# Whole-tile output stores, and v loads issued from ScalarE's queue, in a fused linear-attention and FFN kernel

## The chip, the cores and the metric

The kernel runs on one core of a Trainium2 chip. The metric is device time in microseconds, as the median of several runs. Below, "the profile" is one traced run of a kernel; its span is some 2 us shorter than the time of the same run, because the time includes the start and end of the launch. TensorE is PE, VectorE DVE, ScalarE ACT, GpSimd POOL, SyncE SP; a "q" after the name is the engine's sequencer.

## The reference

```python
# q, k, v: (4, 8, 768, 64) float32; lam: (8,)
for b in range(12):                       # blocks of 64 tokens
    intra = (qb @ kb.T * Dmask) @ vb      # decayed causal attention inside the block
    inter = (qb * lam_pow) @ kv_state     # what earlier blocks left
    out[:, :, sl] = intra + inter
    kv_state = lam_block * kv_state + (kb * rev_pow).T @ vb
x = out.transpose(0, 2, 1, 3).reshape(3072, 512)
h = x @ w_in                              # 512 -> 2048
g = h + sin(alpha * h) ** 2 / (alpha + 1e-9)
return g @ w_out                          # (3072, 512) float32
```

## The kernel before

The attention is cut into 24 units u (a batch row, four heads, 256 tokens); four units make a group g of 512 tokens for the FFN, and a group gives four output tiles (g, m) of 128 rows by 512 columns. The order of all work is fixed by a long list of items such as `ld.12.2:S` (the v load of unit 12 on SyncE) or `st.3.1.0:S` (the store of half 0 of tile 3.1). Each engine takes its own items strictly in order.

The parts that matter here:

```python
stagep = ...tile_pool(name="stage", bufs=8)     # q, k, v as loaded
outp   = ...tile_pool(name="outp", bufs=4)      # output tiles "ob"

def load(u, j, **_):
    ...
    loads[u, j] = nc.sync.dma_start(out=tl[:]..., in_=src[b, ...]...)

def outev(u, c, eng, **_):                      # attention output -> xt, tokens as (two, i)
    copy(eng, xt[g][:, 2 * hh:2 * hh + 2, bb, c, :],
         okv[u][c][:, 0:2 * P].rearrange("p (hp i) -> p hp i", hp=2))

def out_rows(g, m):
    ...
    return out[r0:r0 + C].rearrange("(p two) d -> two p d", two=2)   # (2, 64, 512)

def store(g, m, par, **_):                      # twice per tile
    nc.sync.dma_start(out=out_rows(g, m)[par],
                      in_=obs[g, m][par * D:(par + 1) * D, :])
```

Partitions 0 to 63 of an output tile hold the even rows, 64 to 127 the odd ones. Therefore a tile goes out in two stores, each to every second row.

## Time and profile before

| | before |
|---|---|
| median time | 215.98 us (216.06 with the run added beside the change) |
| span of the profile | 213.8 us |
| TensorE busy | 204.0 us, 95% |
| DMA issues from SyncE for output | 46 of 128 KB, and the last tile's pieces |
| first tile of group 4 copied at | 184.4 us; from there to the end 29.4 us |

The busy share says how full an engine is over the whole span; the chain says what the end depended on. Here TensorE is full, so a change elsewhere can help little. For the comparison I divide the span at the start of the copy of output tile 4.0 (read from VectorE's timeline): what lies ahead of it is called the middle, what follows it the tail.

### The profile page before, as it was taken

The numbers are of one execution on the slowest core, as the hardware profiler recorded it, in microseconds if no ns is written. First come the engines' busy times: TensorE is split into PE (matmuls) and PEld (weight loads), VectorE is DVE, ScalarE is ACT, GpSimd is POOL, SyncE is SP. The second block draws the span as 40 slices with busy tenths as digits, with TensorE's granted clock in tenths as the row PEclk, the third lists the DMA queues.
The fourth block names the chain that finished last, engine by engine and source line by source line (L and its number), as shares of the span: only waits on it lengthen the run. The fifth ranks groups of instructions, "written<-read, shape, count | busy, mean of one in ns | idle before, by whom it ended". The sixth has DMA issues, their size and how long they took to land.

```text
span 213.8 us, 5465 instructions
## 1 busy us (share of the span) xinstructions
PE 204.0 (95%) x2104; PEld 110.1 (51%) x2132; DVE 129.8 (61%) x235; ACT 123.5 (58%) x244; POOL 141.4 (66%) x208
## 2 busy tenths in 40 slices
PE   7989999999999999999799999999999999999993
PEld 5767544457744554455444554454454444444463
DVE  3885798159599845778667785626884626441120
ACT  3563984077899839986394496936635659131001
POOL 5488389689797999999898996709841728030000
PEclk9999999999999999999999999999999999999999
DMA  5999999999999999989899997520610000171624
GB/s 144 293 235 196 187 204 271 282 291 289 200 205 202 248 213 289 208 103 199 218 268 133 223 179 198 92 49 0 132 44 3 0 0 0 35 179 35 147 51 98
DMA packets 64009, 33.92 MB, mean 159 GB/s; under 512 B 19680, under 2 KB 61040, under 8 KB 63984
## 3 DMA queue, kind: packets, MB, share of 16 engines
q1 hardware_dynamic: 59568, 29.31, 62.5%
q0 software_dynamic: 4224, 4.19, 12.4%
q8 instruction: 16, 0.26, 0.5%
q10 hardware_dynamic: 192, 0.07, 0.2%
q14 instruction: 9, 0.07, 0.1%
HBM read 27.28 MB, written 6.29 MB: 157 GB/s over the span
## 4 chain that ended last, share of the span: by engine, by line
PE 67%; POOL 12%; DMA 10%; issue 3%; ACT 2%; SPq 2%; DVE 2%; POOLq 0%; ACTq 0%
PE ops L525 27%; PE hps L482 24%; DMA w_out_sb<-in_moe_w_out_dram 4%; PE bz L564 3%; DMA QT<-KD 2%; PE okv L460 2%; POOL KD L300 2%; POOL kvbd L425 2%; PE sp L368 2%; PE bz L588 2%; DMA st_v<-in_v_dram 2%; POOL QL L300 2%; POOL kvx L421 2%; PE pt L327 2%; SPq L259 2%
## 5 line engine op out<-in xcount | busy, mean ns | idle before, releaser
L482 PE MATMUL hps<-xt,w_in_sb 128*128 128x512 bf16 (+1 forms) x404 | 86.4, 362 | 0.6 <-issue 0.2
L525 PE MATMUL ops<-w_out_sb,gall 128*128 128x512 bf16 x352 | 83.2, 379 | 2.1 <-issue 1.3
L516 DVE SCALAR_TENSOR_TENSOR gall<-s,r_sb,hps 128x512 bf16<-128x512 bf16 x96 | 68.3, 744 | 23.3 <-POOL s L511 11.7
L502 ACT ACTIVATE s<-hps,alpha_sb 128x512 bf16<-128x512 f32 x96 | 63.2, 688 | 25.7 <-PE hps L482 25.1
L482 PEld LDWEIGHTS <-w_in_sb 128*128 128x128 bf16 x416 | 39.8, 98 | 40.6
L511 POOL TENSOR_TENSOR s<-s 128x512 bf16<-128x512 bf16 x35 | 36.3, 1045 | 36.3 <-ACT s L502 35.6
L525 PEld LDWEIGHTS <-gall 128*128 128x128 bf16 x368 | 34.6, 98 | 39.9 <-issue 0.6
L378 DVE TENSOR_TENSOR ST<-sp,mask 128x512 bf16<-128x512 f32 x48 | 31.9, 684 | 4.4 <-PE sp L368 4.2
L509 ACT ACTIVATE s<-s 128x512 bf16<-128x512 bf16 x51 | 31.6, 634 | 1.0 <-DVE gall L516 0.4
L284 DVE COPY ob<-ops 128x512 f32<-128x512 f32 (+1 forms) x13 | 8.6, 659 | 29.2 <-PE ops L525 23.6
L300 POOL TENSOR_TENSOR QL<-st_q,E 128x512 bf16<-128x512 f32 x23 | 23.9, 1042 | 3.6 <-DVE alpha_sb L574 2.2
L300 POOL TENSOR_TENSOR KD<-st_k,R 128x512 bf16<-128x512 f32 x22 | 22.9, 1042 | 3.5 <-DMA st_k<-in_k_dram 1.8
L425 POOL TENSOR_TENSOR kvbd<-kvx,LBD 128x256 bf16<-128x256 f32 x32 | 19.6, 612 | 2.5
L282 ACT COPY ob<-ops 128x512 f32<-128x512 f32 (+2 forms) x13 | 7.1, 547 | 22.4 <-PE ops L550 12.0
L282 ACT CAST xt<-okv 128x256 bf16<-128x256 f32 x29 | 9.8, 374 | 11.8 <-PE okv L460 11.8
L421 POOL TENSOR_TENSOR kvx<-kva,kvs 128x128 f32<-128x128 f32 x32 | 14.7, 460 | 1.2 <-ACT kva L282 1.0
L284 DVE CAST xt<-okv 128x256 bf16<-128x256 f32 x19 | 7.7, 420 | 11.5 <-PE okv L460 11.5
L282 ACT COPY kva<-kvp 128x128 f32<-128x128 f32 x26 | 6.4, 273 | 9.9 <-PE kvp L400 8.9
L368 PE MATMUL sp<-QT 64*64 64x128 bf16 x384 | 9.9, 219 | 1.3 <-DMA QT<-KD 1.3
L282 ACT COPY QT<-pt 128x512 bf16<-128x512 bf16 x9 | 5.2, 591 | 9.8 <-PE pt L327 9.7
L460 PE MATMUL okv<-ST,VB 64*64 64x128 bf16 x384 | 9.9, 220 | 0.0
L282 ACT CAST VB<-st_v 128x512 bf16<-128x512 f32 x14 | 8.6, 625 | 1.9 <-DMA st_v<-in_v_dram 1.8
(57 smaller groups left out, 127.1 us busy)
## 6 DMA issues: line engine op xcount, KB each, us to landing
st_q<-in_q_dram SPq DMA_DIRECT2D x24, 256.0 KB, 4.8
st_k<-in_k_dram SPq DMA_DIRECT2D x24, 256.0 KB, 5.0
st_v<-in_v_dram SPq DMA_DIRECT2D x24, 256.0 KB, 4.6
out_dram<-ob SPq DMA_DIRECT2D x46, 128.0 KB, 2.8
w_in_sb<-in_moe_w_in_dram POOLq DMA_DIRECT2D x4, 512.0 KB, 7.7
w_out_sb<-in_moe_w_out_dram POOLq DMA_DIRECT2D x4, 512.0 KB, 11.9
QT<-QL SPq DMA_TRANSPOSE x16, 4.1
QT<-KD SPq DMA_TRANSPOSE x16, 3.4
```

Source lines behind the costliest of these rows:

```text
L282: nc.scalar.copy(out=out, in_=in_)
L284: eng.tensor_copy(out=out, in_=in_)
L300: eng.tensor_tensor(out=t[:], in0=stage[u, j][:].rearrange("p h two e -> p two h e"), in1=tab[:, :, hh * HH:(hh + 1) * HH].unsqueeze(3).to ...
L378: nc.vector.tensor_tensor(out=stm[u][:, hd], in0=sps[u][hd][:], in1=mask[:].unsqueeze(2).to_broadcast([P, 2, 2, P]), op=ALU.mult)
L421: eng.tensor_tensor(out=t[:], in0=x, in1=prev[:], op=ALU.add)
L425: eng.tensor_tensor(out=kvbd[u, c][:], in0=x.unsqueeze(2).to_broadcast([P, 2, 2, D]), in1=LBD[:, 2 * hh:2 * hh + 2, :].unsqueeze(3).to_bro ...
L482: f1mm[g, f] = nc.tensor.matmul(out=hps[g, f][:].rearrange("p (b i) -> p b i", b=2)[:, bs] .rearrange("p b i -> p (b i)"), lhsT=w_in_sb[:, ...
L502: nc.scalar.activation(out=s1[g, f][:], in_=hps[g, f][:], func=ACTF.Sin, scale=alpha_sb[:, f:f + 1])
L509: nc.scalar.activation(out=s2[g, f][:], in_=x[:], func=ACTF.Square)
L511: eng.tensor_tensor(out=s2[g, f][:], in0=x[:], in1=x[:], op=ALU.mult)
L516: nc.vector.scalar_tensor_tensor(out=gall[g][:, f, :], in0=s2.pop((g, f))[:], scalar=r_sb[:, f:f + 1], in1=hps.pop((g, f))[:], op0=ALU.mul ...
L525: nc.tensor.matmul(out=ops[g, m][:], lhsT=gall[g][:, f, m * P:(m + 1) * P], rhs=w_out_sb[:, f, :], start=(f == 0), stop=(f == NFC - 1))
```

## The change

The intent is to relieve SyncE, which issues 150 loads, transposes and half stores: one store in place of two, and 15 of its v loads handed to another queue.

```diff
-        loads[u, j] = nc.sync.dma_start(
+        queue = nc.scalar if j == 2 and u > 8 else nc.sync
+        loads[u, j] = queue.dma_start(
...
-    def store(g, m, par, **_):
-        nc.sync.dma_start(out=out_rows(g, m)[par], in_=obs[g, m][par * D:(par + 1) * D, :])
+    def store(g, m, _i, **_):
+        nc.sync.dma_start(out=out_rows(g, m), in_=obs[g, m][:])
```

In the order list the 23 items of second halves (`st.g.m.1:S`) are deleted. Nothing else moves: the sequences of the other four engines in the list are the same, except that ScalarE meets the v loads where they stand between its own items.

## The prediction

> **What bounds the kernel now.** I read the page's span and engine shares first, then its chain, then a table of busy time by stage, then SyncE's issues and the waits for output buffers.
>
> ```profile
> span 213.8 us, 5465 instructions
> PE 204.0 (95%) x2104; PEld 110.1 (51%) x2132; DVE 129.8 (61%) x235; ACT 123.5 (58%) x244; POOL 141.4 (66%) x208
> PE 67%; POOL 12%; DMA 10%; issue 3%; ACT 2%; SPq 2%; DVE 2%; POOLq 0%; ACTq 0%
> ```
>
> TensorE is busy 95% of the span, so nothing can be gained beyond some 10 us, and much can be lost: its instruction order is fixed, so whatever arrives late for it is added to the time. The chain has SyncE's sequencer (SPq) at 2%, about 4 us. That is all that fewer issues could remove directly.
>
> The stages (window, us, then PE, PEld, DVE, ACT, POOL busy, clock, DMA share, GB/s):
>
> ```profile
> 58.00:81.00 23.00, 22.47 (x292) 11.64 (x294) 17.53 (x30) 18.05 (x39) 20.72 (x30) 1.00 1.03 222
> 81.00:100.00 19.00, 18.68 (x194) 9.28 (x197) 14.00 (x22) 16.92 (x35) 18.53 (x30) 1.00 0.92 196
> 100.00:116.00 16.00, 14.46 (x193) 7.73 (x192) 10.47 (x19) 9.99 (x19) 14.84 (x24) 1.00 1.13 214
> 116.00:150.00 34.00, 33.53 (x322) 16.79 (x318) 21.57 (x36) 21.38 (x40) 24.34 (x37) 1.00 0.61 123
> 150.00:185.00 35.00, 34.63 (x254) 16.67 (x258) 20.04 (x32) 19.95 (x35) 17.82 (x22) 1.00 0.12 27
> 185.00:213.00 28.00, 25.23 (x148) 13.14 (x147) 7.78 (x13) 3.00 (x6) 2.08 (x2) 1.00 0.47 104
> ```
>
> From 58 to 116 us the 16 DMA engines are about fully booked (0.92 to 1.13), and POOL with them; later there is room. In that stage the chain, in order of time, runs through transfers (start, us, what):
>
> ```profile
> 79.94 4.26 DMA st_v<-in_v_dram
> ...
> 102.03 2.79 DMA st_k<-in_k_dram
> ...
> 110.00 5.34 DMA QT<-KD
> ```
>
> A delay of transfers there reaches TensorE at once. I set each landing against its first consumer: the k load of unit 19 has 0.1 us to spare, the transposed k of unit 16 0.04, unit 17's 1 to 1.4, unit 12's 2.8; the rest of this stage has 2 to 18.
>
> Stores (SyncE's timeline: start, us, what; the transfer list; the waits):
>
> ```profile
> 81.79 1.74 SPq L540 DMA_DIRECT2D out_dram<-ob  x1
> 83.58 0.59 SPq L259 DMA_DIRECT2D st_v<-in_v_dram  x1
> 84.22 1.18 SPq L540 DMA_DIRECT2D out_dram<-ob  x2
> 85.44 1.31 SPq L345 DMA_TRANSPOSE QT<-KD  x1
> ...
> 185.11 23.61 SPq L540 DMA_DIRECT2D out_dram<-ob  x20
> ```
>
> ```profile
> out_dram<-ob SPq DMA_DIRECT2D x46, 128.0 KB, 2.8
> ```
>
> ```profile
> DVE ob L284 <- DMA out_dram<-ob: 2.9, 1, 2.9
> ```
>
> 20 of the 46 stores are issued after 185 us, in a bunch, because SyncE waited 29.4 us for the first output tile of group 4. The ring of output tiles (`ob`, four buffers) already made VectorE wait 2.9 us for a store's landing. A slower store will lengthen that wait.
>
> **What the Trainium skill says.** (1) "DMA: Bandwidth & Descriptors", section "Why a DMA increments its semaphore by 16 and not by 1": a transfer from SyncE or ScalarE uses k engines, the largest k up to 16 that divides the slowest dimension larger than 1 of both access patterns; on this path these are the lowest-numbered k. The trace of before agrees as far as it goes: its loads carry the pattern 4 x 128, its stores 64 rows of 2048 B, both divisible by 16, and all spread. No run here has shown a small k yet. (2) The same page, "Queues, rings and completion order": each engine takes a queue's descriptors in ring order. So a transfer queued behind a long share of one engine waits for that share. (3) "SBUF — State Buffer", section "Door 1: The DMA port swizzle": 64 partitions reach only 8 of 16 ports. The trace agrees: in the tail, with stores alone, a 2 KB packet lasts 153 ns (median after 184 us in the packet records) and the flow stays at 188 to 222 GB/s, while the shortest, uncrowded 2 KB packets last about 85 ns. (4) The first page's "Rules for kernel authors" calls two transfers to disjoint partition halves no use and advises one 128-partition transfer; this is presumably the intent of the change, but its form matters.
>
> **The change, part by part.**
> *Removed*: 23 of 46 row stores. At a median of 588 ns each, 23 x 0.59 = 13.5 us of SyncE. Most lies in waiting time or the tail; what could come off the chain is two or three issues near 76 to 101 us, 1 to 2 us.
>
> *Moved*: 15 v loads (units 9 to 23), about 0.5 us each: 7.5 us off SyncE, at most 1 to 2 us off the chain; and 7.5 us onto ScalarE, which is busy 18.05 of 23 us in the first stage. The issues take completion semaphores in turn out of eight, and wait, where the records show it, for the reused one; so ScalarE now also waits for a transfer eight issues back. Its stream has the v loads of units 14, 15 and 16 in a row near 74.4 us, before the output copy of tile 1.0; the one eight before the last (the q/k loads of unit 14) landed at 76.3 us. I put 2 to 4 us on ScalarE here, part of it on TensorE's path, and call the two halves of the move even.
>
> *The new store*: the destination is viewed as (2, 64, 512), since odd and even rows cannot be merged into one stride. Its slowest dimension is 2. By (1), k = 2: engines 0 and 1 each carry 64 rows of 2 KB, and 14 engines nothing. Estimate from before's packets: 64 x 85 ns = 5.4 us in place of some 0.7 to 1.2 us for both halves over 16 engines. Issue to landing alone: today's 2.3 us in the tail, of which about 0.65 is data, becomes 1.6 + 5.4 = 7 us.
>
> *Middle stage.* On engines 0 and 1 from 58.8 to 116 us: about 26 loads x 32 packets x 27.5 ns = 23 us; 20 transposes x 32 x 18 ns = 11.6 us; eight stores x 5.4 = 43 us. That is 78 us of work in 57. Going through it: the first two stores (58.8, 70.4) meet spare time, +1 to 2 us; three stores at 81.8 to 84.2 put 16 us before the transposes of unit 12, whose spare is 2.8 plus some idle time, together +8; two at 100.8 and 104.9 put 9 us more before loads and transposes without spare, +8; one at 114, +2; those at 125 and later have 8 us spare or more, +0. Sum about +20.
>
> *Tail.* SyncE issues the stores of 4.0, 3.2, 3.3, 3.1 at 185 to 187 us. At 5.4 each they land, in the old clock, at 192, 198, 203 and 208.6. The copy of tile 4.1 needs the buffer of 3.1: it slips from 189.9 to 208.7 and holds the PSUM bank that the first matmul of tile 5.0 needs (196.5 before). TensorE stands for 13 us. Six more stores follow on two engines: 210.8 + 6 x 5.4 = 243.2, and the last small piece lands about 244. That is +30 on 213.8.
>
> *Sum*: 216 + 20 + 30 - 2 = 264; I take 262, as delays in the middle give the backlog time to drain.
>
> **Rivals.** A: the store spreads over 16 engines after all (the lowering splits differently). Then 256 KB over all ports lands in the same time as one half, SyncE is relieved, and ScalarE's waits eat most of it: 212 to 218. For it: the skill's rule is not seen in this trace. Against: rows 2p and 2p+1 are apart by one row in DRAM but by 64 partitions in SBUF, so there is no common outer dimension of 16. B: k = 2, but the middle stage hides it (loads have up to 18 us spare, v loads have their own ring): only the tail counts, 216 + 26 to 31 = 242 to 247. C: k = 2 and each descriptor takes 153 ns even alone: 9.8 us per store, ten in the tail are 98 us, about 300 us. Against: the 85 ns packets. D: ScalarE becomes the bound by its waits for semaphores; with A this would give 218 to 224, with k = 2 it adds to the sum.
>
> **Range and chances.** k = 2 about nine in ten. Within it, 4.9 to 5.8 us per store gives +26 to +35 in the tail, and the middle +5 to +35. So 236 to 292 holds about eight in ten. Outside k = 2 the time is near today's: faster 0.03, same 0.08, slower 0.89.
>
> **What would show it.** Right: full-tile stores with a median landing of 7 us or more, in the tail 10 to 20; a low flow (near 50 GB/s) after 185 us with a low mean DMA share, since two of 16 engines work; VectorE's wait for `ob` by stores at 15 us or more; TensorE idle near 197 us. In the middle, score matmuls (line 368) waiting for transposes near unit 12 and units 16 to 19. Wrong: a landing near 2.5 us in the tail means k = 16 and rival A; PE at 93% or more up to 185 us means B; waits of ScalarE before its load issues as the longest mean D.

## The result

The change took 273.89 us (median of 4 runs, 271.31 to 274.45), against 216.06 us. The ratio is 1.266 (95% interval 1.258 to 1.275). Ratios here are the mean time of one kernel's fast runs over that of the other's of the same rounds, so not quite the ratio of the medians. The prediction of 262, with a range of 236 to 292, held.

The page after, in the same order as it was read before: span, engine shares, the rows of clock and DMA share over 40 slices, and the chain.

```profile
span 272.5 us, 5428 instructions
PE 215.9 (79%) x2104; PEld 115.1 (42%) x2132; DVE 130.1 (48%) x235; ACT 123.5 (45%) x244; POOL 141.5 (52%) x208
PEclk9999999999996699689986999999999999976555
DMA  6999999999979629675979997511000011111121
DMA 37%; PE 35%; SPq 12%; POOL 5%; ACT 4%; issue 3%; DVE 0%; ACTq 0%; POOLq 0%; DVEq 0%
```

All engines but TensorE do the same work as before; it takes 59 us more of waiting. The chain has moved from TensorE (67% before) to transfers and SyncE's sequencer. The last ten slices of the DMA row read 1 or 2 tenths, while the kernel does little other than store: something is moving data, and most of the 16 engines are not. The clock row, all 9 before, drops while TensorE waits.

The same stages as before (window, its us, busy time of PE, PEld, DVE, ACT, POOL, clock, DMA share, GB/s):

```profile
58.00:81.00 23.00, 21.44 (x274) 11.61 (x278) 18.20 (x31) 17.60 (x36) 17.93 (x25) 1.00 1.07 168
81.00:100.00 19.00, 12.19 (x62) 5.27 (x62) 3.94 (x7) 8.26 (x17) 9.33 (x14) 0.73 0.70 154
100.00:116.00 16.00, 9.32 (x65) 4.25 (x65) 6.34 (x10) 8.45 (x17) 9.34 (x17) 0.84 0.92 92
116.00:150.00 34.00, 26.23 (x308) 13.78 (x312) 18.21 (x32) 13.46 (x28) 21.95 (x36) 0.87 0.92 134
150.00:185.00 35.00, 34.63 (x316) 17.20 (x320) 21.32 (x34) 24.18 (x44) 23.93 (x33) 1.00 0.77 113
216.00:255.00 39.00, 28.38 (x149) 14.91 (x149) 7.83 (x12) 2.37 (x4) 2.08 (x2) 0.86 0.13 48
```

TensorE loses 6.8 us of 19, 6.7 of 16 and 7.8 of 34 between 81 and 150 us; from 150 to 213 us it is full again. In the last window the DMA share of 0.13 is about two engines of sixteen (0.125).

The flow in that window, in 40 slices of about one microsecond (GB/s), from the transfer view:

```profile
GB/s 0 12 25 45 45 51 51 51 51 51 51 51 51 51 51 51 51 51 49 53 49 53 49 53 49 53 49 53 49 53 49 53 49 53 49 53 49 53 49 51
```

A flat 51 GB/s, whatever the kernel does: 256 KB at that rate are 5.1 us. A second, independent sign is in the semaphore records. Where every transfer is spread over 16 engines, each reports 16 landings. In the profile of the change a store of 4.0, issued at 216.46 us, has three updates of its semaphore: one at 217.39, two at 224.30 and 224.35. The totals agree: a semaphore with 17 transfers, three of them whole stores, has 233 updates, which is 17 x 16 less 3 x 13. (Because of this count the page gives no landing times for the change.) In the store bunch a 2 KB packet lasts 84 ns, against the 85 assumed.

Who waited, in the whole span (us in total, times, longest):

```profile
DVE ob L282 <- DMA out_dram<-ob: 39.4, 5, 14.7
ACT ob L280 <- DMA out_dram<-ob: 38.3, 3, 19.9
...
ACT ob L280 <- DMA st_k<-in_k_dram: 8.8, 1, 8.8
...
PE sp L366 <- DMA QT<-KD: 6.5, 1, 6.5
```

The output copies now wait for stores, where only one wait of 2.9 us was before. The third line is ScalarE standing at a v load, its copy of tile 1.0 behind it. The fourth is TensorE waiting for transposed operands.

VectorE's timeline at the end (start, us, what, in brackets the idle time before it and what ended it):

```profile
224.48 0.69 DVE L282 COPY ob<-ops 128x512 f32<-128x512 f32 x1 [6.07 <-DMA out_dram<-ob]
...
239.83 0.69 DVE L282 COPY ob<-ops 128x512 f32<-128x512 f32 x1 [9.58 <-DMA out_dram<-ob]
244.98 0.69 DVE L282 COPY ob<-ops 128x512 f32<-128x512 f32 x1 [4.46 <-DMA out_dram<-ob]
250.20 0.69 DVE L282 COPY ob<-ops 128x512 f32<-128x512 f32 x1 [4.53 <-DMA out_dram<-ob]
```

Together with ScalarE's copies (234.7, 255.2, 260.3 us), one copy starts every 5.1 us: each takes the buffer that a store has just left. The tail runs at the pace of the stores.

SyncE's timeline where the middle loses most (start, us, what):

```profile
91.87 5.33 SPq L538 DMA_DIRECT2D out_dram<-ob  x3
97.24 8.02 SPq L343 DMA_TRANSPOSE QT<-KD  x1
```

The three stores are the trio (tiles 1.1, 0.3 and 0.2) whose first halves were issued between 81.8 and 84.8 us before. The transpose behind them is the one of unit 12 that took 1.31 us to issue before. Now its issue alone lasts 8.02 us.

### The profile page after: what moved, and what is told of

It reads as the page before. It is cut to its first block, busy times and chain, and to the rows that moved or that the text cites. A ratio compares the mean times of both kernels' runs of the same rounds, so it can differ in the third digit from the quotient of the medians.

```text
span 272.5 us, 5428 instructions
## 1 busy us (share of the span) xinstructions
PE 215.9 (79%) x2104; PEld 115.1 (42%) x2132; DVE 130.1 (48%) x235; ACT 123.5 (45%) x244; POOL 141.5 (52%) x208
## 4 chain that ended last, share of the span: by engine, by line
DMA 37%; PE 35%; SPq 12%; POOL 5%; ACT 4%; issue 3%; DVE 0%; ACTq 0%; POOLq 0%; DVEq 0%
PE hps L480 18%; DMA out_dram<-ob 17%; PE ops L523 12%; SPq L257 9%; DMA QT<-KD 8%; DMA st_q<-in_q_dram 6%; DMA st_v<-in_v_dram 4%; DMA st_k<-in_k_dram 2%; SPq L538 2%; ACT s L500 2%; PE okv L458 2%; PE sp L366 1%; POOL QL L298 1%; POOL KD L298 1%; PE okv L444 1%
## 5 line engine op out<-in xcount | busy, mean ns | idle before, releaser
L480 PE MATMUL hps<-xt,w_in_sb 128*128 128x512 bf16 (+1 forms) x404 | 89.6, 371 | 7.8 <-DVE gall L514 5.7
L523 PE MATMUL ops<-w_out_sb,gall 128*128 128x512 bf16 x352 | 85.8, 388 | 2.6 <-issue 1.4
L480 PEld LDWEIGHTS <-w_in_sb 128*128 128x128 bf16 x416 | 40.4, 99 | 50.1 <-issue 11.4
L523 PEld LDWEIGHTS <-gall 128*128 128x128 bf16 x368 | 35.2, 99 | 42.4 <-issue 4.4
L298 POOL TENSOR_TENSOR QL<-st_q,E 128x512 bf16<-128x512 f32 x23 | 23.9, 1042 | 5.7 <-DMA st_q<-in_q_dram 3.4
L366 PE MATMUL sp<-QT 64*64 64x128 bf16 x384 | 10.6, 230 | 7.9 <-DMA QT<-KD 6.5
L444 PE MATMUL okv<-QT,kvbd 128*128 128x128 bf16 x80 | 9.5, 232 | 7.3 <-ACT xt L280 6.8
L548 PE MATMUL ops<-w_out_sb,gall 128*128 128x128 bf16 (+1 forms) x48 | 6.3, 318 | 8.3 <-DVE ob L282 8.3
L444 PEld LDWEIGHTS <-kvbd 128*128 128x128 bf16 x80 | 6.9, 104 | 12.7 <-issue 8.6
```

The lines of the kernel that those rows point to most:

```text
L298: eng.tensor_tensor(out=t[:], in0=stage[u, j][:].rearrange("p h two e -> p two h e"), in1=tab[:, :, hh * HH:(hh + 1) * HH].unsqueeze(3).to ...
L444: nc.tensor.matmul(out=okv[u][c][:, hp * P:(hp + 1) * P], lhsT=sts[c][:, hp].rearrange("p two e -> p (two e)"), rhs=QT[:, 0, :, hp, half[c ...
L480: f1mm[g, f] = nc.tensor.matmul(out=hps[g, f][:].rearrange("p (b i) -> p b i", b=2)[:, bs] .rearrange("p b i -> p (b i)"), lhsT=w_in_sb[:, ...
L523: nc.tensor.matmul(out=ops[g, m][:], lhsT=gall[g][:, f, m * P:(m + 1) * P], rhs=w_out_sb[:, f, :], start=(f == 0), stop=(f == NFC - 1))
```

## The experiments

All medians below are of 4 runs (6 for the last two, 3 for the kernel before). The column "copy of 4.0" is from each profile, and so is the tail.

| run | median us | ratio to before | copy of 4.0 | tail |
|---|---|---|---|---|
| before | 215.98 | | 184.4 | 29.4 |
| the change | 273.89 | 1.266 | 215.7 | 56.8 |
| e1_store_only | 272.48 | 1.258 | 210.7 | 56.9 |
| e2_vloads_only | 225.06 | 1.044 | 193.0 | 29.8 |
| e3_natural_both | 224.74 | 1.041 | 195.3 | 29.3 |
| e4_natural_store | 216.61 | 1.001 | 185.5 | 29.4 |
| e5_mid_only | 246.17 | 1.140 | 214.7 | 29.7 |
| e6_tail_only | 251.64 | 1.165 | 193.6 | 57.0 |
| e7_tail_order | 261.00 | 1.208 | 215.5 | 43.1 |
| e8_natural_halves | 217.74 | 1.007 | 186.5 | 29.4 |
| e9_outer_four | 238.05 | 1.106 | 204.4 | 32.2 |
| e10_vloads_part | 220.33 | 1.021 | 189.2 | 30.0 |
| e11_moving_natural | 316.29 | 1.467 | | |
| e12_moving_tail | 317.16 | 1.470 | | |

My theory: the destination view (2, 64, 512) confines a whole-tile store to two DMA engines, and all of the loss follows from stores of 5.1 us, in the middle through transfers queued behind them and in the tail through the four output buffers. Rivals: a large store as such is slow; the v loads on ScalarE do the harm; the tail is paced by the lower clock.

### e1_store_only: the stores alone

```diff
-        queue = nc.scalar if j == 2 and u > 8 else nc.sync
+        queue = nc.sync
```

> The whole-tile stores of the change, with all v loads back on SyncE's queue. Theory (stores run on two DMA engines, 5.1 us each, everything else follows): the tail from the copy of tile 4.0 to the end stays at about 57 us (29 before), and the middle loses less than the +31 of the change, since ScalarE no longer waits for completion semaphores behind slow stores: +18 to +28; total 258 to 270. Rival (the v loads on ScalarE do the harm): below 225.

Measured: 272.48 us, 2.5 us above the expected range, and only 1.4 us less than the change, which is within the spread of the runs. The tail is 56.9 us. (The profile fell on a quick run, 2.9 us under the median: its span is 267.6 us.) The stores alone bring nearly the whole loss; the v loads are not needed for it. TensorE's wait for the transposes of unit 12 is here undiluted:

```profile
PE sp L366 <- DMA QT<-KD: 19.1, 4, 14.3
```

One wait of 14.3 us, close to the three stores in front of that transpose (3 x 5.1 = 15.3 us).

### e2_vloads_only: the v loads alone

```diff
-        loads[u, j] = nc.sync.dma_start(
+        queue = nc.scalar if j == 2 and u > 8 else nc.sync
+        loads[u, j] = queue.dma_start(
```

> The kernel before with only the 15 v loads moved to ScalarE's queue, half stores as before. Theory: 214 to 220, a loss of at most 4 us, as ScalarE waits at the v loads of unit 9 (near 44 us) and of unit 16 (near 75 us), each by a few us. Rival (the v loads do the harm): over 235, with ScalarE's output copy waiting for a load by 8 us or more as in the change.

Measured: 225.06 us, 9.3 us over the kernel before of the same rounds (215.75). That is well above my "at most 4", and well below the rival's 235. In the change this cost is almost fully hidden behind that of the stores (273.89 against 272.48). The trace shows where a good part of it comes from. ScalarE's timeline:

```profile
80.03 1.79 ACTq L260 DMA_DIRECT2D st_v<-in_v_dram  x3
81.86 0.58 ACT L283 COPY ob<-ops 128x512 f32<-128x512 f32 x1 [4.11 <-DMA st_k<-in_k_dram]
```

At these three loads ScalarE stands 4.1 us. The records say for what: the first waits for a completion semaphore whose last user, a q load, landed at 80.01, and the third for one whose last user, a k load, landed at 81.38; they are issued at 80.03 and 81.40. Neither has anything to do with the v buffers. The same happens near 44 us at the v load of unit 9. In the records of this kernel, eight completion semaphores serve all transfers of SyncE and ScalarE, and a new user is issued only after the last one has landed.

### e10_vloads_part: fewer of the v loads

```diff
+        queue = nc.scalar if j == 2 and u > 8 and u not in (9, 10, 14, 15, 16) else nc.sync
```

> The kernel before with the v loads on ScalarE's queue only for units 11 to 13 and 17 to 23; those of units 9, 10, 14, 15 and 16, where ScalarE waited for the semaphore of a transfer eight issues back, stay on SyncE. Theory (the 9 us that the v loads alone cost come from ScalarE's waits at those five places, not from issuing on ScalarE): 215.5 to 219. Rival (each load on ScalarE costs about as much, 9 us over 15): 221 to 223.

Measured: 220.33 us, half of the cost gone, between the range of the theory and that of the rival. By the time alone, then, neither is shown: ten of fifteen loads at an equal share of the 9.3 us would cost 6.2, and 4.6 were measured. The trace shows that the kind of wait was right and the list of places was not. With those five loads away, ScalarE stands at others (ScalarE's timeline):

```profile
107.54 0.69 ACT L503 ACTIVATE s<-hps,alpha_sb 128x512 bf16<-128x512 f32 x1 [4.27 <-DMA st_k<-in_k_dram]
```

The v load just before it was issued at 107.10; its semaphore's last user had landed at 107.08. Another stands 2.9 us at 115.7. Whether every bit of the remaining 4.6 us is such waits was not tried.

### e3_natural_both and e4_natural_store: one large store with a large outer dimension

The copy to `xt` puts the tokens into natural order, so the 128 rows of a tile are one run in DRAM:

```diff
-        copy(eng, xt[g][:, 2 * hh:2 * hh + 2, bb, c, :],
-             okv[u][c][:, 0:2 * P].rearrange("p (hp i) -> p hp i", hp=2))
+        copy(eng, xt[g][:, 2 * hh:2 * hh + 2, bb, c, :]
+             .rearrange("p hp (i two) -> p hp two i", two=2),
+             okv[u][c][:, 0:2 * P].rearrange("p (hp two i) -> p hp two i", hp=2, two=2))
...
-        return out[r0:r0 + C].rearrange("(p two) d -> two p d", two=2)
+        return out[r0:r0 + C]
...
```

(The last cut gives the pieces of the last tile the same rows.) e3 keeps the v loads on ScalarE, e4 puts them back on SyncE.

> Both parts of the change, but tokens are put into natural order when the attention output is copied to xt, so that one store is 128 rows in a row and its slowest dimension is 128. Theory (the outer dimension of 2 did it, not the size of 256 KB): a store lands in about 2.5 us in the tail over 16 engines, the flow after 185 us is again 100 GB/s or more, total 212 to 220. Rival (one large store as such is slow, or the v loads): stays over 240.

> As the natural-order run, but with all v loads on SyncE's queue. Theory: 211 to 217, at least as fast as with the v loads on ScalarE; perhaps 1 to 2 us under the kernel before, since 23 issues of 0.6 us fall away and the last bunches of stores read all 128 partitions. Rival (one large store is slow): over 235.

Measured: e4 216.61 us, e3 224.74 us. A store of the same 256 KB, also one per tile, costs nothing when it spreads. Its row in the transfer list of e4 (count, size, us from issue to landing):

```profile
out_dram<-ob SPq DMA_DIRECT2D x23, 256.0 KB, 2.3
```

That is quicker than the half stores of before (2.8 us for 128 KB), and each of these stores has 16 semaphore updates. The rival "a large store as such is slow" falls. e3 is above its range by 5 us and equal to e2: with the stores repaired, what is left of the change is the cost of the v loads, which I had underrated.

### e8_natural_halves: the control

> Control: the kernel before with the natural token order alone, two half stores at their old places, v loads on SyncE. Theory: the permuted copy costs nothing that shows, within 1.5% of the kernel before. If it is slower, that is the price that the natural-order runs carry.

Its edit is that of the copy to `xt`, with the rows viewed as "(two p) d" so that two half stores remain. Measured: 217.74 us, 0.7% over before (interval 1.002 to 1.012). The permuted copy on ScalarE lasts 450 ns in place of 374. The single store is 1.1 us under this control (216.61), but the two come from different sets of rounds and the intervals overlap, so a gain is not shown. The version with one store is equal to the kernel before (ratio 1.001, interval 0.995 to 1.007) and does not beat it.

### e9_outer_four: the dose

```diff
-        return out[r0:r0 + C].rearrange("(p two) d -> two p d", two=2)
+        return out[r0:r0 + C].rearrange("(p a) d -> a p d", a=4)
...
```

(The cut keeps the rows of the last tile's pieces as they were.)

> The change with one thing altered: the destination rows are viewed as (4, 32, 512) instead of (2, 64, 512), for all tiles stored whole. The rows land permuted, so the result is wrong on purpose; bytes, descriptors of 2 KB and instructions are the same. Theory (the engines used are the largest divisor up to 16 of the outer dimension): four engines, 64 x 2 KB / 25.6 GB/s / 2 = 2.6 us per store instead of 5.1, the flow in a bunch of stores near 102 GB/s instead of 51; the tail from the copy of tile 4.0 takes 30 to 35 us; total 226 to 238. Rival (a whole-tile store to rows that are not in one run is slow whatever its outer dimension): within 5 us of the change.

Measured: 238.05 us, 0.05 us past the upper end of what was expected; the result was wrong, as meant. Flow while the stores of the tail run:

```profile
GB/s 25 18 43 43 61 93 100 100 100 107 100 103 103 100 107 100 100 103 103 100 103 103 100 107 100 100 107 100 100 107 100 100 107 100 100 107 100 100 107 100
```

Twice the flow of the change, about 103 GB/s. A store here has five semaphore updates (one at once, four as data lands) in place of three. The size of the outer dimension sets the number of engines: by the landings, 2 gave two, 4 gave four, 128 gave sixteen. The tail is nearly healed (32.2 us), since ten stores of 2.6 us fit into 29 us; the middle is still 11 us slower than with the v loads alone.

### e5_mid_only and e6_tail_only: one stage at a time

```diff
+        if g < 3:        # e5; g >= 3 in e6
+            nc.sync.dma_start(out=out_rows(g, m), in_=obs[g, m][:])
+            return
+        for par in range(2):
+            nc.sync.dma_start(out=out_rows(g, m)[par], in_=obs[g, m][par * D:(par + 1) * D, :])
```

> The change, with the (2, 64, 512) store only for groups 0 to 2; groups 3 to 5 store two halves at the same place. Theory (losses of middle and tail add up): tile 4.0 is copied near 215 us as in the change, then 29 to 32 us to the end; total 243 to 250. Rival (one of the stages causes the loss of the other): the tail still takes over 40 us.

> The mirror image: groups 0 to 2 store two halves at the same place, groups 3 to 5 in the (2, 64, 512) form. Theory: the middle is near that of the kernel with only v loads moved (tile 4.0 copied at 184 to 192 us), the tail takes 55 to 58 us; total 241 to 250. Rival (v loads on ScalarE make the middle slow): tile 4.0 copied after 205 us.

Measured: e5 246.17 us with a tail of 29.7; e6 251.64 us (1.6 us over its range) with a tail of 57.0 and the copy of 4.0 at 193.6 (expected 184 to 192), where e2 has 193.0. Above e2's 225.06 the stores of the middle add 21.1 us and those of the tail 26.6, in sum 47.7; the change adds 48.8. To about 1 us the two losses add up and do not depend on each other. (e2 was measured in another set of rounds; the kernel before differed by 0.2 us between the two.)

### e7_tail_order: another order of the same stores

```diff
-st.4.0.0:S st.3.2.0:S st.3.3.0:S st.3.1.0:S
+st.3.1.0:S st.3.2.0:S st.3.3.0:S st.4.0.0:S
```

> The change, with the stores of tiles 3.1, 3.2 and 3.3 put ahead of that of 4.0 in SyncE's order, so that they go as soon as their tiles are copied (near 189, 200 and 212 us) instead of waiting for 4.0 at 216. Nothing else. Theory (the tail is a queue of ten stores of 5.1 us on two engines): two of them, 3.1 and 3.2, are out before the bunch and 3.3 nearly so, tile 4.1 no longer waits for the buffer of 3.1, the tail shrinks by 10 to 16 us; total 258 to 265. Rival (the tail is paced by the lower clock of TensorE or by something else than the queue of stores): within 3 us of the change.

Measured: 261.00 us, and the tail falls by 13.7 us to 43.1. Only the order of four items changed. So the tail is a queue of stores. The rival, that the clock paces it, falls.

### e11_moving_natural and e12_moving_tail: attempts at a faster version

```diff
-                rhs=xt[g][:, c, bs].rearrange("p b c i -> p (b c i)"),
+                rhs=xt[g][:, c, bs].rearrange("p b c (two i) -> p (b c) i two", two=2),
...
```

e11 also has the contiguous store of e4, with v loads on SyncE; e12 adds the order of e7.

> Single whole-tile stores, v loads on SyncE, with natural token order made where FFN1 reads xt (a strided moving operand) instead of where xt is written. Theory: stores as good as in the other natural-order run, without its slower copies to xt; if the strided read costs TensorE nothing, 212 to 215, a little faster than before. Rival: the strided read slows the 404 FFN1 matmuls (362 ns now), and each 10 ns more is 4 us.

> As the previous run, with the stores of tiles 3.1, 3.2 and 3.3 ahead of that of 4.0 in SyncE's order. Theory: the wait of VectorE for the buffer of tile 3.1 near 190 us (2.9 us in the kernel before) goes away, and the end comes 0 to 2 us sooner than without it.

Measured: 316.29 and 317.16 us, a clear miss. The row of FFN1's matmuls in e11 (count | busy us, mean ns | idle before):

```profile
L480 PE MATMUL hps<-xt,w_in_sb 128*128 128x512 bf16 (+1 forms) x416 | 190.1, 608 | 0.0
```

A matmul lasted 608 ns in place of 362, and the stage around it is paced by that. The Trainium skill's "SBUF — State Buffer", section "Door 1: The DMA port swizzle", has a box on 16-byte lines: reading on past a line each time costs bandwidth. Neighbours in the new order lie 128 bytes apart, so this run agrees, but the mechanism itself was not isolated. Whether the order of e7 helps a healthy kernel stays open: in e11 no copy waits for a store, so in e12 there was nothing to gain. A variant that permuted the stationary operand was not built, because only one free dimension is allowed there. No version tried beats the kernel before.

## Why the prediction was right, step by step

**Two engines: right.** The rule taken from the Trainium skill, "DMA: Bandwidth & Descriptors", section "Why a DMA increments its semaphore by 16 and not by 1", held at 2, 4 and 128. (The records list the fastest dimension first: in the prediction's "4 x 128" the slowest is 128.) Which two engines they are, the trace does not tell.

**A store of 5.4 us: right in kind, 0.3 us high.** It was 5.1 us at 51 GB/s. 84 ns per packet times 64 would be 5.4; packets overlap a little. Rival C (153 ns per packet, 9.8 us) falls, rival A (spread after all) too.

**The tail, +30: measured +27.4, with one wrong link.** I let the copy of tile 4.1 wait for the store of 3.1, taking the four buffers in rotation, and TensorE stand 13 us at tile 5.0. In the trace the copy of 4.1 starts at 224.48, when the store of 4.0 has landed (224.35), and that of 4.2 at 229.56, when 3.2 has (229.48). Buffers went out in the order in which the program gives them back, not in rotation. TensorE ran on to the last tile. The end is nearly the same, because ten stores on two engines set it, whoever waits.

**The middle, +20: measured +31.3; the trio of stores is the term that was mis-sized.** The delay against before at the first score matmul of a unit, from TensorE's records (us):

| | unit 11 | 12 | 16 | 17 | 18 | 21 |
|---|---|---|---|---|---|---|
| the change | 4.1 | 20.1 | 21.7 | 29.8 | 31.3 | 31.3 |
| e1, stores alone | 1.5 | 16.3 | 17.0 | 21.0 | 23.9 | 26.3 |

My terms were for stores, so e1 tests them (its profile is of a quick run, and may be some 3 us short in all). The first two stores, +1 to 2: 1.5, right. The trio before unit 12, +8: 14.8, nearly twice. The later ones, +8, +2 and 0: 9.3 in sum, right, not taken apart further. I had credited unit 12 with its spare 2.8 us "plus some idle time"; in e1 TensorE stands 14.3 us there for 15.3 us of stores, so almost nothing was absorbed.

In the change the path is another one. Its three longest stands of TensorE in the middle (TensorE's timeline):

```profile
88.35 0.48 PE L444 MATMUL okv<-QT,kvbd 128*128 128x128 bf16 x3 [6.75 <-ACT xt L280]
112.00 0.64 PE L366 MATMUL sp<-QT 64*64 64x128 bf16 x16 [6.46 <-DMA QT<-KD]
143.00 1.86 PE L480 MATMUL hps<-xt,w_in_sb 128*128 128x512 bf16 x4 [5.66 <-DVE gall L514]
```

Only the second is the wait for transposes behind the trio. The first ends before the trio is issued (91.9 us, ten later than before): ScalarE stands 8.8 us at the v load issued at 86.10, whose semaphore's last user, a q load behind the store of 74.3 us, landed at 86.08. In e2, with half stores, the same stand is 4.1 us. So the 16.0 us between units 11 and 12 are 6.75 of ScalarE's wait, 6.46 of the trio's, and the rest mostly the halved clock from 83.6 to 93.9 us. The third is the same kind: ScalarE stands 5.7 us at the v load issued at 141.06, whose semaphore's last user, a transposed k, landed at 141.03. The delay of 8.1 us at unit 17 thus equals my +8 for the pair of stores by luck; the score matmuls of units 16 to 19, which I had named as a sign, do not wait for transposes there. Rival B (the middle hides it) falls: e5 alone adds 21.1 us to e2.

**The v loads, "even": wrong.** Alone they cost 9.3 us, not 0. I had seen the semaphore waits near 75 us and set them at 2 to 4 us. I did not go through the other places, and e10 shows that the waits move on when some are removed. In the total it did not show (1.4 us between e1 and the change): where ScalarE's wait comes first, the wait for the trio's transposes behind it is shorter, 6.5 us in place of 14.3. What rival D gave for the kernel with repaired stores, 218 to 224, is nearly met: e3 at 224.74.

**The clock: not foreseen.** TensorE's busy time grew from 204.0 to 215.9 us for the same matmuls. The granted clock fell to half for 10.2, 6.8, 6.8, 3.4 and 27.2 us of the span, each time after TensorE had stood idle. The Trainium skill's "TensorE: Matmul & The Clock Gate", section "Part 1: The HAM clock gate (the “warmup” mystery)", says that idle TensorE falls to half the clock; the records agree. How much of it lay on the path that sets the end was not separated.

The sum came out 12 us low: the middle 11 us more than allowed (in e1's profile the trio is some 7 of it; the change's middle is 5 us longer than e1's, by the v loads and by the quick run that e1's profile fell on), a tail 3 us shorter, and the rest rounding of mine (I had taken 262 in place of my sum of 264, and 2 us of gain that did not come).

## What to carry to other kernels

Before merging two transfers into one, look at the outermost dimension of both access patterns: one that is small leaves most DMA engines unused (2 gave two engines here, 4 gave four), and what is queued behind it on these engines waits. Moving a load to a compute engine's queue is not free even if its issue lasts 0.4 us, because that engine, in its order, also takes over every wait of the load. And to price a slow transfer, ask what stands behind it in its queue and which buffers it holds, not only whether its own data are needed soon.

## What the Trainium skill lacked or had wrong

- "DMA: Bandwidth & Descriptors", "Why a DMA increments its semaphore by 16 and not by 1": the rule for the number of engines held (2 and 4). The page has no measured rate of a confined transfer; its "Specifications" give about 27 GiB/s (29 GB/s) for an engine, and here it is 25.6 GB/s per engine (51 GB/s with two, 103 with four).
- Same page, "Rules for kernel authors": the row that advises one 128-partition transfer for two halves does not point to the row "Use all 16 engines" of the same table, which warns of a small outermost dimension. Both are needed: in the view at hand the single store cost 57 us (e1, 272.48 against 215.75); in a spreading view it was 1.1 us under the halves (216.61 against 217.74), not clear of noise.
- Same page, "Issuing engines are not separate DMA queues": it says that issuing from several engines saves issue time. It does not say that an issuing compute engine can stand for the semaphore of an unrelated transfer (that the wait is the issuing sequencer's, the page says elsewhere): 15 loads moved cost 9.3 us here, with single waits of 4.1 and 4.3 us.
- "Perfetto Trace Analysis", "DMA Instruction — HWDGE (DVE, Sync)", mentions a descriptor buffer that can fill, but no page gives a time for an issue behind a crowded engine: a transpose's issue lasted 8.02 us behind three confined stores, against 1.31 before. A full buffer would explain it; that was not shown.
- "SBUF — State Buffer", "Door 1: The DMA port swizzle": the box on 16-byte lines has no figure for a matmul's moving operand. Here 608 ns against 362, with elements 128 bytes apart.
